# All down products moved behind the up products and put in seven-product form, with the tokens between them kept in DRAM

## The chip, the cores and the metric

The kernel runs on one core of a Trainium2 chip. The metric is the device time of one execution in microseconds (us), the median of the runs shown. Profiles are of one execution each, with times from the start of its span.

## The reference

Softmax attention with a tanh cap on the scores, over 4 batches, 12 heads, 448 tokens and heads of 64; then, per batch, a token mixing of rank 32 and a feed-forward layer 768 -> 3072 -> 768 with a relu.

```
scores = q @ k.T / 8;  scores = cap * tanh(scores / cap)
x = softmax(scores) @ v                     # heads side by side: 448 x 768 per batch
u = x + (x.T @ U @ V).T
out = u + relu(u @ w_ch1) @ w_ch2           # w_ch1 768 x 3072, w_ch2 3072 x 768
```

U, V, w_ch1 and w_ch2 come as 64-bit floats and are turned into 32-bit ones on the core (`convert`: one operation of ACT and two of DVE per block). Each 32-bit operand of the feed-forward layer is split in a high and a low half, and a product is the sum of three matmuls: high by high, high by low, low by high.

## The kernel before, in words

**Planning.** Every piece of work is a task with an estimated duration, the engines that may run it, the buffers that it takes and a priority (a lower number goes first). `simulate` (L133) places all tasks in time, an engine taking the ready task of the lowest number whose buffers have room, and `emit` (L230) writes the instructions out in that order, so each engine's order is fixed when the program is built. Buffers of one tag are handed out in the order in which they were declared, from the first of their pools that has room; a pool with `after` opens when all buffers that are to come from the named pools are done. `Pool.part` makes a pool out of one large tile of another.

**Attention** (`four`, `normalize`, `mixin`, to about 190 us). For each head pair `scores` (L488, PE), tanh (L495) and exp (L506, ACT), the product with v (L522, L531, L546), and DVE's sums of the exponentials over the key tiles (L552). The 448 keys are three tiles of 128 and a remainder of 64. Below head pair 12 (`ALONE`) the remainder is added into the sums by DVE; from 12 on PE adds it in a second set of matmuls with ones (L588). `fill` gives PE 14 small matmul turns (L405) at the start. Beside this the first feed-forward weights and the first token operands are made, as far as buffers allow: four token operands (tag `x`: one in `wx`, three in `xe`) and four weight operands (tag `ws` in `wp`).

**Feed-forward** (`moe`, L772). The batches are taken in two pairs, (0, 1) and (2, 3), each in 12 chunks of 256 hidden units. Up (`up_seven`): a chunk is a 2 x 2 block product (two batches by two blocks of 128 hidden units, the 768 inputs in two halves) done with seven products in place of eight, 9 matmuls of 448 columns each (L867): 63 per chunk. The products run in the order of `ORDER`; results are gathered in PSUM and in `cx` tiles by ACT (`keep`) and DVE (`plus`). Bank "a" takes products 1, 6, 7 and 4 one after the other, and is read in between.

Down, first pair (`down`): in plain form, 72 matmuls per chunk (L948), run between the up products of the next chunk, two outputs behind each product. The raw w1 and w2 of a chunk are loaded (L724, SP, 768 KB each, two buffers of tag `wr`), converted into `wa` tiles, written to DRAM for the second pair (L728, ACT's queue, 384 KB each), and split. Outputs go onto the result tiles `u` in SBUF by a DVE addition (L953), or, two in five, by a copy of ACT and an accumulating DMA of POOL's queue (L961).

Down, second pair: for ten of the twelve chunks, two chunks at a time, in seven-product form (`down_seven`, 126 matmuls, L1075), its operands made from the kept weights and from the relu'd tokens that stay in SBUF (tag `gq`); the last two chunks in plain form behind all up products. The 72 down products of the first pair's last chunk stand between the two pairs.

The operands of a pair (`operands`, L674) are seven tiles `x` of 6 rows x 448; terms 5, 6, 3 and 7 are formed in one `wr` buffer.

Of the kernel before, what the change touches and what calls it, by code (L numbers as in the profile page):

```python
# [29 lines left out]
QUADS = 5  # L30
PORDER = 2, 3, 1, 6, 5, 7, 4
# [6 lines left out]
FILL, FIRST = 14, 3  # L38
# [3 lines left out]
class Pool:  # L42


    def __init__(self, name, bufs, after=(), space=None, side=None, shared={}, within=None, parts=None):
        self.name, self.bufs, self.after, self.space, self.side = name, bufs, after, space, side
# [15 lines left out]
    def part(self, b, opened):  # L62
        if self.whole is None:
            p, g = self.within
            self.whole = opened(p).tile([128, NP, S], self.parts[0], tag=g, name=self.name, bufs=1)
        return self.parts[1][self.at(b)][b.slot](self.whole)
# [12 lines left out]
class Task:  # L79
    __slots__ = ("durs", "eng", "fn", "bufs", "prio", "mode", "lat", "wait", "next", "i", "begin", "at", "ready", "lock")  # L80
# [8 lines left out]
class Plan:  # L89
# [16 lines left out]
    def task(self, durs, fn, r=(), w=(), prio=0, mode=None, lat=None, begin=0, lock=False):  # L106
# [4 lines left out]
        t.lat, t.eng = lat, None  # L111
# [21 lines left out]
    def simulate(self):  # L133
# [6 lines left out]
        events, out, now = [], [], 0  # L140
# [34 lines left out]
        def start(t, e):  # L175
# [16 lines left out]
            heapq.heappush(events, (now + cost + OVER.get(e, 0) + (LAT[e] if t.lat is None else t.lat), 2, t.i, "d"))  # L192
# [37 lines left out]
    def emit(self, tc, order, first):  # L230

        engines = {"DVE": self.nc.vector, "POOL": self.nc.gpsimd, "ACT": self.nc.scalar}
        with tc.manual_schedule(), ExitStack() as st:

            def opened(p):
                if p.pool is None:
                    for q in p.after:
                        if q.stack:
                            q.stack.close()
                            q.stack = None  # L240
                    p.stack = st.enter_context(ExitStack())
# [28 lines left out]
class Build(Plan):  # L270
    def __init__(self, tc, qk, v, u, vv, w1, w2, cap, ident, out):
# [12 lines left out]
        self.xe = Pool("xe", {"x": 3, "cx": 2}, after=(self.pre,), shared={"st": "cx"})  # L284
# [4 lines left out]
        self.gx = [Pool("gx", {"g": 1}, after=(self.an, self.aq), within=w, shared={"gp": "g"}) for w in ((self.aq, "xx"), (self.an, "rb"))]  # L289
# [122 lines left out]
    def attention(self):  # L412
# [6 lines left out]
        self.gw = Pool("gw", {"gq": 3}, after=(self.wx,), within=(self.wx, "x"), parts=(F32, {"gq": thirds}))  # L419
        self.g0 = Pool("g0", {"gq": 3}, after=(self.ua,), within=(self.ua, "u0"), parts=(F32, {"gq": thirds}))  # L420
        self.gz = Pool("gz", {"gp": 3}, after=(self.g0,), within=(self.ua, "u0"), parts=(F32R, {"gp": thirds}))
        self.g1 = Pool("g1", {"gq": 1, "ta": 1, "vs": 1}, after=(self.ua,), within=(self.ua, "u1"), parts=(F32, {
            "gq": thirds, "ta": [lambda t: t[:, 2, :DM // 2]], "vs": [lambda t: t[:, 3:6]]}))
# [13 lines left out]
    def four(self, p):  # L437
# [73 lines left out]
        for h in range(2):  # L511
# [24 lines left out]
            for i, o in enumerate(os):  # L536
# [23 lines left out]
                if p < ALONE:  # L560
# [9 lines left out]
    def normalize(self, p):  # L570
# [5 lines left out]
        rest = p >= ALONE  # L576
# [97 lines left out]
    def operands(self, bs, order, prio):  # L674
# [3 lines left out]
        pools = (self.wx, self.xe, self.late) if bs[0] == 0 else (self.xe, self.late)  # L678
# [34 lines left out]
    def block(self, which, f, first, begin, prio):  # L713

        nc = self.nc
        a = self.buf("wa", [128, DM], F32, self.wp, self.late)
        if not first:
            self.task({"SP": 350}, lambda: nc.sync.dma_start(out=a.t, in_=self.kept[which, f]),
                r=[("kept", which, f)], w=[(a, 0)], lat=4000, prio=prio)
            return a  # L720
        raw = self.buf("wr", [128, 2 * DM], I32, self.wq)
# [4 lines left out]
        def keep():  # L726
            d = self.kept[which, f] = self.dp.tile([128, DM], F32, tag="kept", name="kept", bufs=2 * NF)
            nc.scalar.dma_start(out=d, in_=a.t)  # L728

        self.task({"SP": 350}, load, w=[(raw, "u"), (raw, "l")], lat=7500, prio=prio, begin=begin)  # L730
        self.convert(raw, lambda: raw.t, a, lambda: a.t, prio, DM)
        self.task({"ACT": 120}, keep, r=[(a, 0)], w=[("kept", which, f)], lat=7000, prio=prio)
        return a

    def strassen_weights(self, c, first, begin, prio):
# [3 lines left out]
        ws = {p: self.buf("ws", [128, 2, K], F32R, self.wp, self.late) for p in ORDER}  # L739
        c, c7 = (self.buf("ta", [128, K], F32, self.wp, self.g1) for _ in range(2))  # L740
# [9 lines left out]
    def weights(self, f, first, begin, prio):  # L750
        tag, pool = ("w1", self.wp) if first or f // CF != 2 * QUADS else ("wl", self.wq)
        w = self.buf(tag, [128, 2, DM], F32R, pool)
        a = self.block(1, f, first, begin, prio)

        def high():
            self.copy(self.nc.scalar, w.t[:, 0], a.t)

        def low(e):
            e.tensor_tensor(out=w.t[:, 1], in0=a.t, in1=w.t[:, 0].bitcast(F32), op=ALU.subtract)

        self.task({"ACT": 840}, high, r=[(a, 0)], w=[(w, 0)], prio=prio)
        self.task({"DVE": 960}, low, r=[(a, 0), (w, 0)], w=[(w, 1)], prio=prio, lock=True)
        return w

    def bank(self):
        return self.buf("mm", [128, 512], F32, self.pm, self.pl)

    def prepare(self, c, first, begin, prio):
        ws = self.strassen_weights(c, first, begin, prio)
        return ws, {c * CF + i: self.weights(c * CF + i, first, begin, prio) for i in range(CF) if first}  # L770

    def moe(self):  # L772


        self.kept, rest = {}, []
        order, pend = 10, None
        for n, bs in enumerate(((0, 1), (2, 3))):
            made = {}
            if not n:
                made[0] = self.prepare(0, True, 60000, ALONE - 90)  # L780
            xs = self.operands(bs, ORDER if n else EARLY, -50 if n else ALONE - 90)
            vs = self.buf("vs", [128, 3, S], F32, self.g1) if n else None
            gq, last, down, turns = {}, None, iter(()), [2] * 7
            for c in range(NCH):
                fs = [c * CF + i for i in range(CF)]
                ws, w1 = made.get(c) or self.prepare(c, n == 0, 0, 3 if n or c < NCH - 2 else -60)
                gs = {}
                four = n and c < 2 * QUADS
                if pend:
                    down, turns = self.down(order, *pend), [2] * 7  # L790
                    pend = None
                elif gq and c % 2 == 0:
                    down = self.down_seven(order, bs, c // 2 - 1, gq, vs)
                    gq = {}
                if n:
                    turns = [2] * 7 if not c else [1 + (i + c) % 2 for i in range(7)]
                if n and c == 0:
                    for _ in down:
                        pass
                    order += 12  # L800
                if four and c % 2 == 0:
# [360 lines left out]
```

## Time and profile before

| | us |
|---|---|
| three runs | 843.48, 842.36, 842.54; median 842.54 |
| profiled execution | 842.78, span 841.0 |

| engine | busy us | share |
|---|---|---|
| PE (matmuls) | 832.0 | 99% |
| PEld (weight loads, beside PE) | 663.2 | 79% |
| DVE | 675.6 | 80% |
| ACT | 498.2 | 59% |
| POOL | 123.5 | 15% |

The DMA engines moved 129.64 MB, 154 GB/s over the span. Busy times are of the engine's instructions and say nothing on what the end waits for; the chain of waits does, followed back from the last instruction. A mean duration in the lines is that of one instruction from start to end, and following instructions overlap a little with it; a list in order of time shows the step from one start to the next.

### The profile page before, as it was taken

The page shows a single profiled execution, that of the slowest core. Times are in us where ns is not written, and L with a number is a line of the kernel's source. Part 1 is how long each engine was busy: PE and PEld are TensorE (multiplying, and loading weights), DVE is VectorE, ACT ScalarE, POOL GpSimd, SP SyncE. Part 2 cuts the span into 40 slices and gives each one's busy share as a digit, 9 for nine tenths or more (in the row PEclk, how much of TensorE's full clock was granted, in tenths as well). Part 3 has the DMA queues.
Part 4 walks back from the last instruction along what each step waited for, and adds up shares of the span by engine and source line. Part 5 has one row for each costly group of instructions (what it writes and reads, how often), then busy time and mean ns, then how long its engine had stood idle before and what let it go on. Part 6 is the DMA issues. An engine that isn't in the chain of part 4 may idle for free.

```text
span 841.0 us, 12164 instructions
## 1 busy us (share of the span) xinstructions
PE 832.0 (99%) x4524; PEld 663.2 (79%) x4524; DVE 675.6 (80%) x1141; ACT 498.2 (59%) x748; POOL 123.5 (15%) x162
## 2 busy tenths in 40 slices
PE   9999999999999999999999999999999999999998
PEld 4343333337899999999999999999999999999997
DVE  4778999659878878887888899698797887978764
ACT  7989999876545544454455445365565555555510
POOL 0111111111111111111111112001121111211200
PEclk9999999999999999999999999999999999999999
DMA  6456554513878867867686747526346263642413
GB/s 228 132 158 208 152 179 121 168 46 117 254 217 220 262 198 216 237 189 214 205 266 160 207 102 192 148 60 157 71 97 152 44 157 78 134 108 44 103 32 131
DMA packets 47612, 129.64 MB, mean 154 GB/s; under 512 B 6178, under 2 KB 23618, under 8 KB 47554
## 3 DMA queue, kind: packets, MB, share of 16 engines
q1 hardware_dynamic: 23024, 79.29, 29.7%
q0 software_dynamic: 17616, 30.71, 20.1%
q10 hardware_dynamic: 6914, 18.88, 5.7%
q8 instruction: 35, 0.57, 0.3%
q14 instruction: 23, 0.19, 0.1%
HBM read 79.28 MB, written 24.47 MB: 123 GB/s over the span
## 4 chain that ended last, share of the span: by engine, by line
PE 95%; DVE 2%; DMA 1%; ACT 1%; issue 1%; POOL 0%; DVEq 0%; POOLq 0%; ACTq 0%
PE mm L867 36%; PE mm L948 24%; PE mm L1075 15%; PE sc L488 8%; PE o L546 6%; PE misc L662 1%; PE o L531 1%; PE misc L585 1%; PE misc L405 1%; DMA rd<-r 1%; PE misc L651 1%; PE misc L635 1%; DVE x L702 1%; DMA rb<-rd 0%; PE misc L588 0%
## 5 line engine op out<-in xcount | busy, mean ns | idle before, releaser
L867 PE MATMUL mm<-x,ws 128*128 128x448 f32 x1512 | 330.7, 366 | 0.8 <-ACT cx L263 0.8
L867 PEld LDWEIGHTS mm<-x,ws 128*128 128x128 f32 x1512 | 283.3, 188 | 27.5 <-ACT cx L263 1.8
L948 PE MATMUL mm<-g,w 128*128 128x448 f32 x864 | 187.0, 366 | 0.0
L948 PEld LDWEIGHTS mm<-g,w 128*128 128x128 f32 x864 | 162.1, 188 | 13.8 <-issue 0.2
L1075 PE MATMUL mm<-g,w 128*128 128x448 f32 x630 | 139.2, 366 | 0.0
L1075 PEld LDWEIGHTS mm<-g,w 128*128 128x128 f32 x630 | 118.3, 188 | 9.7
L263 ACT ACTIVATE st<-mm 128x448 f32<-128x448 f32 x109 | 59.2, 543 | 80.7 <-PE mm L948 48.7
L961 POOL DMA_DIRECT2D u<-st x60 | 51.7, 862 | 272.3 <-ACT st L263 272.3
L953 DVE TENSOR_TENSOR u<-u,mm 128x448 f32<-128x448 f32 x108 | 66.1, 618 | 29.3 <-PE mm L948 28.9
L488 PE MATMUL sc<-qk 64*128 64x448 f32 (+1 forms) x384 | 77.4, 571 | 0.4 <-ACT th L495 0.4
L506 ACT ACTIVATE th<-th,capt 128x1792 f32<-128x1792 f32 x42 | 75.3, 1792 | 0.8
L495 ACT ACTIVATE th<-sc 128x896 f32<-128x896 f32 x80 | 69.6, 915 | 5.1 <-PE sc L488 4.9
L1098 POOL DMA_DIRECT2D u<-st x45 | 38.9, 864 | 211.6 <-ACT st L263 174.1
L488 PEld LDWEIGHTS sc<-qk 64*128 64x128 f32 (+1 forms) x384 | 27.6, 175 | 41.3 <-issue 18.1
L546 PE MATMUL o<-th,vn 128*64 128x448 f32 x280 | 57.9, 548 | 0.0
L263 ACT ACTIVATE cx<-mm 128x448 f32<-128x448 f32 x42 | 22.9, 546 | 57.4 <-PE mm L867 49.3
L702 DVE TENSOR_TENSOR ws<-ta,ws 128x384 fp32r<-128x384 f32 x96 | 52.8, 554 | 3.1 <-ACT ws L263 2.2
L263 ACT ACTIVATE ws<-ta 128x384 fp32r<-128x384 f32 x57 | 29.5, 520 | 34.6 <-PE mm L867 22.6
L317 DVE SCALAR_TENSOR_TENSOR wa<-wa,wr 128x768 int32<-128x768 int32 (+2 forms) x50 | 46.6, 932 | 4.0 <-ACT wa L309 3.3
L263 ACT ACTIVATE ws<-wa 128x384 fp32r<-128x384 f32 x51 | 26.0, 520 | 39.5 <-PE mm L867 39.5
L552 DVE TENSOR_TENSOR es<-es,th 128x896 f32<-128x896 f32 (+1 forms) x36 | 39.1, 1086 | 11.6 <-ACT th L506 10.9
L309 ACT ACTIVATE wa<-wr 128x768 f32<-128x768 f32 (+2 forms) x50 | 44.3, 888 | 6.9 <-DVE cx L880 1.9
(123 smaller groups left out, 932.3 us busy)
## 6 DMA issues: line engine op xcount, KB each, us to landing
wr<-in_w SPq DMA_DIRECT2D x48, 768.0 KB, 6.7
u<-st POOLq DMA_DIRECT2D x105, 224.0 KB, 4.2
kept<-wa ACTq DMA_DIRECT2D x48, 384.0 KB, 6.4
wa<-kept SPq DMA_DIRECT2D x28, 384.0 KB, 3.7
qk<-in_qk SPq DMA_DIRECT2D x23, 448.0 KB, 4.1
wr<-kept SPq DMA_DIRECT2D x20, 384.0 KB, 4.0
vn<-in_v SPq DMA_DIRECT2D x12, 448.0 KB, 3.9
rb<-rd POOLq DMA_DIRECT2D x24, 224.0 KB, 3.8
```

The costliest lines, as they stand in the source:

```text
L263: e.activation(out=out, in_=in_, func=func)
L317: nc.vector.scalar_tensor_tensor(out=a_t().bitcast(I32), in0=a_t().bitcast(I32), scalar=3, in1=raw_t()[:, 0::2], op0=ALU.logical_shift_lef ...
L488: nc.tensor.matmul(ps.t[out, a, :S], qks[c].t[hd, 1, 128 * t:min(S, 128 * t + 128)], qks[c].t[hd, 0], start=True, stop=True)
L495: nc.scalar.activation(out=th.t[:, j], in_=ps.t[:, :, :S], func=AF.Tanh, scale=(self.half if t == 3 else self.qsc) if raw else 1.0)
L506: nc.scalar.activation(out=th.t, in_=th.t, func=AF.Exp, scale=self.capt)
L546: nc.tensor.matmul(o.t[64 * a:64 * a + 64, :S], vn.t[:, 3 * i + t, a], th.t[:, j, a], start=False, stop=t == 2)
L702: e.tensor_tensor(out=lo, in0=src(), in1=hi.bitcast(F32), op=ALU.subtract)
L867: nc.tensor.matmul(ps.t[:, :S], ws[p].t[:, wi, sl], xs[p].t[:, xi, d], start=fresh and n == 0, stop=n == 8, skip_group_check=not fresh)
L948: nc.tensor.matmul(ps.t[:, :S], w1[f].t[:, wi, sl], g[b, f].t[:, gi], start=f == fs[0] and i == 0, stop=f == fs[-1] and i == 2)
L953: nc.vector.tensor_tensor(out=u.t[:, d], in0=u.t[:, d], in1=ps.t[:, :S], op=ALU.add)
L961: nc.gpsimd.dma_start(out=u.t[:, d], in_=st.t, accum_op=ALU.add)
L1075: nc.tensor.matmul(ps.t[:, :S], w[:, wi, k, sl], g[gi][:, k], start=fresh and n == 0, stop=n == 5, skip_group_check=not fresh)
```

## The change

The feed-forward layer has three stages: all up products of the first pair, all up products of the second pair, and then all down products. The relu'd tokens of both pairs are written to DRAM (`mid`, 224 KB per block, POOL's queue) and read back in the down stage. Down goes over three groups of two sets of four blocks (512 hidden units each); in a group each of the seven products is done for both pairs and three output tiles, 12 matmuls each, all in seven-product form. The raw down weights are converted at places set by `SECONDS`: 4 blocks in the first stage, 12 in the second, 8 in the first down group; they are kept in DRAM in another layout (`quads`). Product 5, which belongs to two outputs, is added to both. Every third output goes by ACT and an accumulating DMA.

Before a chunk's last up product (4) the next chunk's first (5) is put by its priority. The remainder of the softmax sums is added by DVE throughout (`RESTS`), the warm-up turns are 11, attention's early pool `pre` has seven score buffers for three. A pool `wg` opens when `pre` is done and holds two more weight buffers and a large tile, in which the fifth token operand lies (`bx`) and later two down weights (`bw`). The planner counts the transfers' time by size (`moved`).

```
-QUADS = 5
-PORDER = 2, 3, 1, 6, 5, 7, 4
+GROUPS = (0, 1), (2, 3), (4, 5)
+EVERY = 3
+SECONDS = (0, 0, 1, 0, 1, 0, 1, 0, 1, 0, 0, 0), (0, 0, 1, 1, 1, 1, 1, 2, 1, 2, 1, 1), (2, 2, 2, 2)
+PORDER = 2, 1, 3, 6, 5, 7, 4
 ALONE = 12
-FILL, FIRST = 14, 3
+RESTS = 24
+FILL, FIRST = 11, 3
...
@@ simulate
+            if t.size:
+                self.moved = max(self.moved, now + cost + 1800) + t.size
+                done = max(done, self.moved + 500)
...
-        self.wp = Pool("wp", {"wa": 2, "w1": 3, "g": 3, "ws": 4, "ta": 3}, shared={"gp": "g"})
+        self.wp = Pool("wp", {"wa": 2, "ws": 4, "ta": 3})
-        self.pre = Pool("pre", {"th": 3, "qk": 2, "es": 2})
+        self.pre = Pool("pre", {"th": 7, "qk": 2, "es": 2})
+        self.wg = Pool("wg", {"big": 1, "wb": 2, "g": 3}, after=(self.pre,), shared={"wa": "wb", "ws": "wb"})
+        self.bx = Pool("bx", {"x": 1}, after=(self.pre,), within=(self.wg, "big"), ...)
+        self.bw = Pool("bw", {"wl": 2}, after=(self.bx,), within=(self.wg, "big"), ...)
...
+        self.wc = Pool("wc", {"wb": 4}, after=(self.late,), within=(self.wp, "ws"))
+        self.wt = Pool("wt", {"wt": 2}, after=(self.late,), within=(self.wp, "wa"))
+        self.cl = Pool("cl", {"gq": 9, "st": 2}, after=(self.xe,))
+        self.cr = Pool("cr", {"wb": 4, "wt": 2, "wl": 1, "wr": 1, "wa": 1, "gq": 2, "g": 4}, after=(self.late,), side="right")
...
@@ four
-                if p < ALONE:
+                if p < RESTS:
@@ normalize
-        rest = p >= ALONE
+        rest = p >= RESTS
...
@@ moe
+                prio = 3 if n or c < NCH - 2 else -60
+                ws = ws or self.strassen_weights(c, n == 0, 0, prio)
+                for _ in range(SECONDS[n][c]):
+                    self.block(1, next(seconds), True, 0, 3)
+                self.up_seven(n, c, xs, ws, order)
+                ws = None
+                order += 21
+        self.down_all(order, seconds)
...
@@ up_seven
+        if not begin:
+            at = iter([order - 4, *at][:1] + list(range(order + 3, order + 21, 3)))
+        cx = {x: self.buf("cx", [128, S], F32, self.xe, *self.rows) for x in ("c22", "c11", "c12")}
...
+        def store(b, j, x):
+            at = n, c // 2, b, j
+            def out():
+                if at not in self.mid:
+                    self.mid[at] = self.dp.tile([128, 2, S], F32, tag="mid", name="mid", bufs=2 * NF)
+                nc.gpsimd.dma_start(out=self.mid[at][:, c % 2], in_=to(x))
+            self.task({"POOL": 1000}, out, r=[key(x)], w=[("mid", at, c % 2)], lat=4000, size=620, prio=-200)
...
@@ down_all
+        for ms in GROUPS:
+            for x, p in enumerate(PORDER):
+                for _ in range(SECONDS[2][x - 3] if ms is GROUPS[0] and x > 2 else 0):
+                    self.block(1, next(seconds), True, 0, prio, (self.cr,))
+                for m in ms:
...
+                    if p == 3:
+                        term(a[m, 1, 0], a[m, 0, 0], ALU.subtract, a[m, 1, 0], size)
+                        s2[m] = self.buf("wt", [128, 2, K], F32, self.wt, self.cr)
+                        term(s2[m], a[m, 1, 1], ALU.subtract, a[m, 1, 0], size)
+                    if p in (3, 5):
+                        ts = self.buf("wt", [128, 2, K], F32, self.wt, self.cr)
...
+                    x = w[p, m] = self.buf("wl", [128, 2, 2, K], F32R, self.bw, self.wq, self.cr)
+                    split(...)
+                for n in range(2):
+                    for m in ms:
+                        at = {2: (1, 0), 3: (1, 1), 1: (0, 0), 6: (0, 1), 7: (1, 0)}.get(p)
+                        if at:
+                            b[(m, n, *at)] = token(m, n, *at)
+                        if p == 6:
+                            term(b01, b11, ALU.subtract, b01, size)
+                            term(b00, b01, ALU.add, b00, size)
+                        if p == 5:
+                            term(b11, b11, ALU.subtract, b00, size)
+                        if p == 7:
+                            term(b10, b10, ALU.subtract, b00, size)
+                        hi, lo = g[p, n, m] = [self.buf("g", [128, 2, S], F32R, self.wg, *self.gx, self.cr) for _ in range(2)]
+                        split(src, ...)
+                for n, bs in enumerate(((0, 1), (2, 3))):
+                    for d in range(3):
+                        fresh = p not in (6, 5, 4)
...
+                        self.task({"PE": 6 * 206 * len(ms)}, products, ..., prio=order, mode="mm")
+                        order += 1
+                        for u, e in onto:
+                            count += 1
+                            self.onto(ps, ..., count % EVERY == 0 and not (last and p in (7, 4)))
```

`split` makes the high half on ACT and the low half on DVE; `term` is one DVE operation; `token` and `weight` are loads on SP's queue.

## Rows read from the trace of the kernel before

**Rows 1.** Span of the core and mean granted clock (1 is full speed).
```profile
core 0: 841.0 us, clock 0.999
```
**Rows 2.** The chain of work that ended last, by engine.
```profile
PE 95%; DVE 2%; DMA 1%; ACT 1%; issue 1%; POOL 0%; DVEq 0%; POOLq 0%; ACTq 0%
```
**Rows 3.** Stretches: PE, PEld, DVE, ACT, POOL busy (instructions), clock, DMA share, GB/s.
```profile
20.00:140.00 120.00, 117.35 (x848) 43.48 (x844) 103.07 (x158) 113.90 (x122) 18.96 (x31) 1.00 0.53 159
...
100.00:191.00 91.00, 90.36 (x681) 33.96 (x685) 70.98 (x114) 80.03 (x86) 14.08 (x24) 1.00 0.42 125
...
260.00:280.00 20.00, 20.00 (x100) 18.35 (x99) 16.17 (x28) 10.17 (x19) 2.59 (x3) 1.00 0.94 274
...
480.00:500.00 20.00, 20.00 (x101) 18.54 (x100) 19.65 (x39) 10.92 (x21) 2.58 (x3) 1.00 0.57 140
...
520.00:540.00 20.00, 20.00 (x101) 18.51 (x99) 12.38 (x24) 7.42 (x14) 2.58 (x3) 1.00 0.82 241
```
**Rows 4.** The chain in order of time: start us, us, what.
```profile
234.92 3.70 PE mm L867 x18
...
482.52 3.66 PE mm L867 x18
...
526.34 27.43 PE mm L867 x135
...
807.93 29.11 PE mm L948 x144
```
**Rows 5.** DVE in order of time: start us, us, line, operation, shapes, count.
```profile
205.33 0.61 DVE L880 TENSOR_TENSOR cx<-cx,mm 128x448 f32<-128x448 f32 x1
205.87 0.55 DVE L695 TENSOR_TENSOR ta<-wa,ta 128x384 f32<-128x384 f32 x1
206.33 0.55 DVE L314 TENSOR_SCALAR wr<-wr 128x768 int32<-128x768 int32 x1
206.80 0.61 DVE L835 SCALAR_TENSOR_TENSOR g<-cx,g 128x448 fp32r<-128x448 f32 x1
207.62 1.09 DVE L614 TENSOR_TENSOR u<-u,rb 128x896 f32<-128x896 f32 x1 [0.21 <-DMA rb<-rd]
208.63 0.55 DVE L702 TENSOR_TENSOR ws<-ta,ws 128x384 fp32r<-128x384 f32 x1
...
213.56 0.97 DVE L317 SCALAR_TENSOR_TENSOR wa<-wa,wr 128x768 int32<-128x768 int32 x1
214.44 0.96 DVE L759 TENSOR_TENSOR w<-wa,w 128x768 fp32r<-128x768 f32 x1
215.31 1.15 DVE L669 TENSOR_TENSOR u<-u,misc 128x448 f32<-128x448 f32 x2
```
**Rows 6.** Groups by line: busy us, mean ns | idle before, releaser.
```profile
L961 POOL DMA_DIRECT2D u<-st x60 | 51.7, 862 | 272.3 <-ACT st L263 272.3
...
L309 ACT ACTIVATE wa<-wr 128x768 f32<-128x768 f32 (+2 forms) x50 | 44.3, 888 | 6.9 <-DVE cx L880 1.9 <-DVE wa L317 1.7 <-DVE ws L702 1.6
...
L263 ACT ACTIVATE g<-gw 128x896 fp32r<-128x896 f32 x19 | 18.0, 948 | 1.5 <-DVE gw L994 1.3
...
L588 PE MATMUL misc<-th,ones 128*32 128x448 f32 x48 | 5.6, 539 | 0.0
```
**Rows 7.** DMA queues (q1 SP, q0 POOL, q10 ACT): packets, MB, share of 16 engines.
```profile
q1 hardware_dynamic: 23024, 79.29, 29.7%
q0 software_dynamic: 17616, 30.71, 20.1%
q10 hardware_dynamic: 6914, 18.88, 5.7%
```
**Rows 8.** The chain's last piece: start us, us, what.
```profile
837.07 0.62 DVE u L953
```
**Rows 9.** Raw weight loads (L724): landing; SP's waits for a buffer (total, times, longest).
```profile
DMA to landing us min/median/max: 5.2/6.7/8.3
...
SPq L724 <- DVE wa L317: 218.7, 45, 12.3
```

More of the change, by code (lines that the diff above doesn't have):

```diff
@@ L139, in simulate @@
         locked = {"DVE": 0, "POOL": 0}
-        events, out, now = [], [], 0
+        events, out, now, self.moved = [], [], 0, 0
         for t in self.tasks:
@@ L240, in opened @@
                             q.stack = None
+                    for q in p.under:
+                        opened(q)
                     p.stack = st.enter_context(ExitStack())
@@ L711, in part, with block @@
         self.task({"DVE": 130 + 1.09 * n}, partial(low, src=src), r=[k, (t, 2 * d)], w=[(t, 2 * d + 1)], prio=prio, lock=True)
-    def block(self, which, f, first, begin, prio):
+    def block(self, which, f, first, begin, prio, only=None):
         nc = self.nc
-        a = self.buf("wa", [128, DM], F32, self.wp, self.late)
+        a = self.buf("wa", [128, DM], F32, *(only or (self.wp, self.late, self.wg)))
         if not first:
-            self.task({"SP": 350}, lambda: nc.sync.dma_start(out=a.t, in_=self.kept[which, f]),
-                r=[("kept", which, f)], w=[(a, 0)], lat=4000, prio=prio)
+            self.task({"SP": 350}, lambda: nc.sync.dma_start(out=a.t, in_=self.kept[f]),
+                r=[("kept", which, f)], w=[(a, 0)], lat=4000, size=1200, prio=prio)
             return a
-        raw = self.buf("wr", [128, 2 * DM], I32, self.wq)
+        raw = self.buf("wr", [128, 2 * DM], I32, *(only or (self.wq,)))
         def load():
@@ L748, in strassen_weights @@
         return ws
[L750 to L763, printed above, removed]
@@ L765, in bank @@
     def bank(self):
         return self.buf("mm", [128, 512], F32, self.pm, self.pl)
-    def prepare(self, c, first, begin, prio):
-        ws = self.strassen_weights(c, first, begin, prio)
-        return ws, {c * CF + i: self.weights(c * CF + i, first, begin, prio) for i in range(CF) if first}
     def moe(self):
-        self.kept, rest = {}, []
-        order, pend = 10, None
+        self.kept, self.quads, self.mid = {}, {}, {}
+        order, seconds = 10, iter(range(NF))
         for n, bs in enumerate(((0, 1), (2, 3))):
-            made = {}
-            if not n:
-                made[0] = self.prepare(0, True, 60000, ALONE - 90)
+            ws = None if n else self.strassen_weights(0, True, 60000, ALONE - 90, (self.wg,))
@@ L823, in moe @@
-        self.last_sums(bs, vs)
-        for x in rest:
-            for _ in self.down(order, *x):
-                pass
-            order += 20
-    def relu(self, b, f, src, key, gs):
-        nc = self.nc
-        tag, pools = ("g", (self.wp, *self.gx)) if b < 2 else ("gp", (self.gz, self.wp, *self.gx))
-        g = gs[b, f] = self.buf(tag, [128, 2, S], F32R, *pools)
-        def low():
-            nc.vector.scalar_tensor_tensor(
-                out=g.t[:, 1], in0=src(), scalar=0.0, in1=g.t[:, 0].bitcast(F32), op0=ALU.max, op1=ALU.subtract)
-        self.task({"ACT": 550}, lambda: self.copy(self.nc.scalar, g.t[:, 0], src(), AF.Relu), r=[key], w=[(g, 0)], prio=-200)
-        self.task({"DVE": 640}, low, r=[key, (g, 0)], w=[(g, 1)], prio=-200)
@@ L905, in up_seven @@
             result(0, 1, "c12")
-            yield
         else:
```

329 lines of the change are left out of this document (100 added, 229 removed).

## The prediction

> **What bounds the kernel now.** I read the views in this order: span and clock, the chain that ended last, the stretches, then the lines and queues that the new stages lean on. The one core takes 841.0 us at a granted clock of 0.999 of full speed [rows 1], so no part of the time is a clock to be won back. The chain of waits is TensorE for 95% [rows 2]. The stretches say the same of the feed-forward part: PE is busy for 20.00 of 20 us with its weight loads at 18.35 to 18.54, while DVE runs from 12.38 to 19.65 of 20 [rows 3]. So what counts there is the number of matmuls times their pitch. The pitch is read from the chain: from 234.92 to 482.52 us lie nine chunks of 135 matmuls (63 up, 72 down), 247.60 / 1215 = 0.2038 us each; a stretch of up products alone gives 27.43 / 135 = 0.2032, the last stretch of down products 29.11 / 144 = 0.2022 [rows 4]. I take 0.2035. That the 135 up products at 526.34 run without a gap and with no down work between them matters for the change: it is the form of its first two stages, though with the weights already in 32 bits.
>
> The attention part (to about 196 us, which is 837.07 less 3150 x 0.2035) is less clear: from 20 to 140 us PE is busy 117.35 of 120 us and ACT 113.90 [rows 3].
>
> The profiled execution took 842.78 us, 1.8 us more than its span; the median of the three runs is 842.54, so both are one number for this purpose. A measurement of this kernel can tell about 0.2% (1.7 us) from no change.
>
> **The matmuls.** Before: up 24 x 63 = 1512; down 12 x 72 = 864 in plain form for the first two batches, 5 x 126 = 630 in seven-product form and 2 x 72 = 144 plain for the others: 3150. After: up 1512 again; down 3 groups x 7 products x 6 outputs x 12 matmuls = 1512: 3024. That removes 126 x 0.2035 = 25.6 us, all of it on the path.
>
> **The attention.** With RESTS at 24 the sums of the remainder rows leave PE: six normalizations lose their second half, whose 48 instructions take 5.6 us [rows 6], some 5.2 us without the overlap of their ends. DVE takes 12 more additions of 896 elements, at 1.01 us each when they follow one another [rows 5] 12.1 us; a fifth token operand (three low halves, 1.6 us) and two weight operands (about 1.9 us) come forward as well, while the two down weights that were converted and split there (2 x 2.2 us) go. Net about 11 us on a DVE that is busy 70.98 of the 91 us from 100 to 191 [rows 3]: it fits. ACT there is at 80.03 of 91. I count the 5.2 us as gained; the bounds are 0 (ACT or DVE takes the place) and 7.2 (the four extra score buffers also remove some 2 of the 2.65 us in which PE idles from 20 to 140 us). Three warm-up turns fewer lie in PE's idle time: nothing, at most 1 us.
>
> By PE's busy share this stage is PE's. The Trainium skill (Perfetto Trace Analysis, Identifying the Most-Contended Engine) holds matmul busy time to be a bad measure and takes the share of weight-load time in its place; by it PE, with 43.48 of 120 us of weight loads here, would not be the bound, ACT at 113.90 would, and the 5.2 us would be worth nothing: 821 us in place of 816. The trace sides with neither wholly, and the case is a rival below.
>
> **First stage: up products of the first pair, no down work between.** A chunk now lasts 63 x 0.2035 = 12.8 us where it lasted 27.5. DVE per chunk, with the steps from one start to the next [rows 5]: two raw blocks 2 x (0.47 + 0.88) = 2.7, four terms and seven low halves 11 x 0.46 = 5.1, three additions 3 x 0.54 = 1.6, a third of a down-weight conversion 0.45: 9.8 of 12.8 us, 77%. That is less than the 19.65 of 20 at 480 us, beside which PE had no gap. The transfers are nearer to their limit. The queues' bytes over their share of the span give 317 GB/s for SP's, 394 for ACT's, 182 for POOL's, which mostly accumulates [rows 7]. Per chunk: two raw blocks of 768 KB 5.0 us, two kept blocks 2.0, a third of a down weight 1.2, and the four stores of relu'd tokens (0.92 MB), an operation that before doesn't have: at ACT's rate 2.3, at POOL's own 5.0. So 10.5 us (82%) or 13.2 us (103%) of 12.8. Before loads the engines to 0.94 of their time in one stretch [rows 3] with PE at 20.00. A plain store has no read of its destination, so I take 2.3; the other end costs at least 0.4 x 11 = 4 us, and more through latency (a rival). POOL issues four stores per chunk at 862 ns [rows 6]: 3.4 of 12.8 us.
>
> The relu'd low halves and plain down weights that go (four and two per 27.5 us) were DVE and ACT work under PE: nothing.
>
> The last product of a chunk writes the bank that an addition of DVE still reads. Down products stood between; now the next chunk's first product does (1.83 us). An operation under way (up to 1.09) and the addition (0.61) [rows 5] make 1.7 us, ahead of what the signals take. I take 0; without that cover it would be 1 us per chunk.
>
> **The seams.** Into the second pair, the 72 down products at 511.77 that covered the new token operands are gone. Two of the seven fit in the spare buffers; five are left, 24 operations x 0.54 = 12.9 us of DVE, with 7 to 10 weight operands (7.4) and six additions (3.2): 23.5 us in the 20 us between the first freed buffer and the last product that needs one. Up to 3 us late, 0 where weights are ready early; I take 2. At the start, chunk 1 now comes 12.8 us after chunk 0, and one raw buffer is held by the token term until its seventh operand: 1. Into the down stage, the last buffers open only when up ends, but three tokens and five operand buffers lie ready, which is half a product, 7.3 us; what is missing is one load, at most the 8.3 us that the longest landing of a larger one took [rows 9], and two splits: 1. In all 4, bounds 0 and 8.
>
> **Down stage.** Per group DVE does 22 weight operations (768 elements) x 0.87 = 19.1, 44 token operations (896) x 1.01 = 44.4, and 32 of 48 evictions x 0.54 = 17.3: 80.8 us beside 504 x 0.2035 = 102.6 us of PE, 79%; the first group converts eight more down weights, 8 x 1.35, 89%. The heaviest products, 6 and 5, take 18.7 and 18.5 us there against 14.7, so they must be prepared ahead; the terms are formed in place in the 14 token buffers, for which products 2 and 1 (8 us each) leave room. I take 0. The end is as before: an eviction of 0.62 [rows 8] and a store.
>
> **Sum.** 842.8 - 25.6 - 5.2 + 4 = 816 us.
>
> **Rivals.**
> (a) Attention gives nothing back, because ACT or the fuller DVE sets it: 821, up to 825 where DVE's 11 us don't all fit. For it: ACT at 95% from 20 to 140 us. Against: from 100 to 191, where the sums go, PE has 90.36 of 91 and ACT 80.03 [rows 3].
> (b) The loop of raw weights sets the first stage. Two buffers serve 2.33 loads per chunk, so one turn may last 11.0 us. It needs a landing, 5.2 to 8.3 us now with a median of 6.7, then ACT's 0.89 and DVE's 0.95 with an operation ahead of each, some 3 us [rows 5, 6, 9]. The 45 waits of SP for a free buffer, 218.7 us, show that it now turns at leisure, 13.8 us [rows 9]. With 8.3 + 3.7 = 12.0 each of some 26 loads costs half a microsecond more: 13 us, 829 us.
> (c) Slower than before: the same loop with landings that grow with the queue, since 3.7 MB in 12.8 us is 286 GB/s, above all that the stretches show (274 at 0.94). At 11 us plus 3 a turn is 14, a chunk 16.3, and 11 chunks cost 39 us: 855. It decides from landings of about 10.1 us (a turn of 13.1, 27 us lost). Against: nothing above 8.3 was seen.
> (d) The ring of nine operand buffers paces the down stage. Half a product (7.3 us of PE) frees four; if terms are not made ahead, product 6 needs ACT 0.95 [rows 6], two low halves 2.0, a weight's 0.9, two evictions 1.1 and four terms 4.0: 9.0 us. With product 5 at 8.9 that is 6.6 us per group, 20 in all, and 7 more for the eight conversions: 843, no change. Against: 14 token buffers let the terms run ahead.
>
> **How the numbers follow.** Forecast 0.60, with 809 to 824 as its own range; (a) 0.12, (b) 0.12, (c) 0.10, (d) 0.06. The 80% range is 809 to 836: it takes in (a) and (b) and leaves out (c) and (d). Faster: 0.60 + 0.12 + 0.12 + a part of (d) = 0.86; the same: the middle of (d), 0.03; slower: (c) and the rest of (d), 0.11.
>
> **What would show it.** PE: 3024 matmuls at 0.203 us. First stage: products back to back, 12.8 us per chunk; DMA share about 0.8, raw landings under 8 us; gaps in PE with raw weights as releaser would show (b) or (c). Attention: first up product about 5 us earlier and no second half of the sums. Seams: single gaps of 1 to 3 us at some 345 and 500 us. Down: PE at 20.00 of 20, DVE at 16 to 18; gaps ahead of products 6 and 5 would show (d). The prediction is wrong if PE has more than 10 us of gaps after the attention, or a pitch other than 0.203.

## The result, and the profile after

The changed kernel takes 828.99 us (median of four runs, 828.35 to 829.72) beside 842.45 (four runs, 841.5 to 843.48): a ratio of 0.984, 95% interval 0.9823 to 0.9857. It is 13.5 us (1.6%) faster, where the forecast was 26.5 us faster, at 816.0. The profiled execution took 828.35 us with a span of 826.6 at a granted clock of 0.993 (before [rows 1]: 841.0 at 0.999).

Stretches of after ("after" is the changed kernel, "before" the other), columns as in [rows 3]:
```profile
20.00:185.00 165.00, 159.53 (x1150) 58.29 (x1148) 144.14 (x216) 154.39 (x169) 25.05 (x42) 1.00 0.46 139
185.00:220.00 35.00, 30.39 (x186) 22.95 (x183) 26.64 (x49) 18.27 (x37) 5.59 (x10) 0.90 0.53 177
220.00:340.00 120.00, 119.39 (x586) 109.30 (x585) 107.05 (x205) 73.22 (x132) 21.57 (x37) 1.00 0.79 275
340.00:380.00 40.00, 39.29 (x193) 35.76 (x192) 39.67 (x83) 25.63 (x50) 7.18 (x12) 1.00 0.57 190
380.00:490.00 110.00, 110.00 (x545) 101.91 (x543) 87.37 (x177) 55.70 (x100) 20.22 (x35) 1.00 0.76 254
490.00:520.00 30.00, 25.75 (x118) 22.79 (x117) 12.42 (x18) 12.11 (x20) 4.47 (x8) 0.94 0.47 168
520.00:620.00 100.00, 100.00 (x493) 92.19 (x492) 95.12 (x117) 48.69 (x65) 14.24 (x16) 1.00 0.92 296
620.00:820.00 200.00, 200.00 (x984) 184.57 (x983) 155.16 (x187) 77.55 (x105) 24.09 (x28) 1.00 0.50 134
```
The first number after the comma is PE. The three long stretches of the feed-forward part (220 to 340, 380 to 490, 520 on) are full, but for 0.61 us in the first. PE is missing in two short ones: 4.61 us from 185 to 220 and 4.25 from 490 to 520, and both have a granted clock below full speed. Attention has lost something too: 5.47 us of idle PE from 20 to 185, where before had 165 - 162.35 = 2.65:
```profile
20.00:185.00 165.00, 162.35 (x1188) 59.92 (x1186) 133.99 (x205) 153.26 (x162) 25.47 (x42) 1.00 0.49 146
```

The end of the chain of waits of after (start us, us, what), which answers to [rows 4, 8], without the steps of `issue` (0.02 to 0.04 us each) and one eviction of 0.63 us:
```profile
355.25 151.67 PE mm L817 x747
507.62 2.10 PE mm L817 x9
509.74 3.54 DMA wb<-quad
513.30 0.85 ACT bw L272
514.18 0.97 DVE bw L908
515.19 307.70 PE mm L963 x1504
```
The pitch is 151.67 / 747 = 0.2030 us for up products. For down products it is 307.70 / 1504 = 0.2046 (eight of the 1512 ran before), or 0.2036 without some 1.5 us at a lower clock at its start. Between them lies a seam of 8.3 us in which 9 + 6 + 2 matmuls ran; a load of a down weight, its high half (L272) and its low half (L908) stand in the chain there. The load starts 0.02 us after the last up product ends, and SP's longest wait ahead of such a load (total, times, longest, us) was for an up product:
```profile
SPq L889 <- PE mm L817: 16.8, 2, 13.6
```
So the buffer that this down weight needed was held by an up weight until then. The end of the kernel is an eviction of 0.62 us, as it was.

PE in order of time at the start of the feed-forward part, after (start us, us, line, operation, shapes, count, idle time before it and its releaser):
```profile
198.63 2.09 PE L817 MATMUL mm<-x,ws 128*128 128x448 f32 x9
205.27 1.10 PE L650 MATMUL misc<-ident,u 64*112 64x64 f32 x16 [4.55 <-DVE u L629]
206.30 3.73 PE L817 MATMUL mm<-x,ws 128*128 128x448 f32 x9
209.96 1.08 PE L666 MATMUL misc<-xx,ust 112*32 112x128 f32 x16
210.97 2.08 PE L817 MATMUL mm<-x,ws 128*128 128x448 f32 x9
```
After 4.55 us without work, nine matmuls take 3.73 us, where they take 2.09 ahead of the hole and 2.08 a little later: the granted clock is 0.50 from 206 to 210 us, the lower of its two levels (1.2 GHz, not 2.4). With the transposes (1.10 for 0.66) and the 16 mixing products (1.08 for 0.65), that is another 2.5 us, so this hole costs some 7.

What DVE, ACT and POOL did around it, same columns, from three views of after:
```profile
204.12 1.09 DVE L629 TENSOR_TENSOR u<-u,rb 128x896 f32<-128x896 f32 x1 [2.25 <-DMA rb<-rd]
```
```profile
204.44 0.55 ACT L272 ACTIVATE cx<-mm 128x448 f32<-128x448 f32 x1 [4.33 <-DMA mid<-cx]
```
```profile
196.84 1.05 POOL L624 DMA_DIRECT2D rb<-rd  x2 [2.35 <-DMA rd<-r]
197.88 0.57 POOL L843 DMA_DIRECT2D mid<-cx  x1
```
Two things come late at once. The last normalization (L629) waits for its reciprocals, a DMA issued at 196.84, and PE's order has its transposes ahead of further up products. Beside that, ACT cannot copy an up product out of PSUM, since both `cx` tiles are held: ACT's wait ends with the landing of a store that was issued at 197.88, and the copy starts at 204.44.

POOL's DMA queue in after, which answers to [rows 7], and landing times of the raw weights and the new store (issue, count, KB each, median us):
```profile
q0 software_dynamic: 14400, 37.82, 17.1%
```
```profile
wr<-in_w SPq DMA_DIRECT2D x48, 768.0 KB, 6.5
mid<-cx POOLq DMA_DIRECT2D x96, 224.0 KB, 4.3
```
By these POOL's queue moves 37.82 MB in 17.1% of 826.6 us, 268 GB/s, where it gave 182 while mostly accumulating. In the first stage PE was busy 119.39 of 120 us with the DMA share at 0.79; raw weights landed at a median of 6.5 us.

### The profile page after: what moved, and what is told of

It is laid out like the page before. It is cut to its first block, busy times and chain, and to the rows that moved or that the text cites. A ratio compares the mean times of both kernels' runs of the same rounds, so it can differ in the third digit from the quotient of the medians.

```text
span 826.6 us, 11913 instructions
## 1 busy us (share of the span) xinstructions
PE 805.9 (97%) x4344; PEld 639.0 (77%) x4344; DVE 676.8 (82%) x1067; ACT 481.1 (58%) x686; POOL 123.0 (15%) x193
## 3 DMA queue, kind: packets, MB, share of 16 engines
q0 software_dynamic: 14400, 37.82, 17.1%
## 4 chain that ended last, share of the span: by engine, by line
PE 59%; DVE 2%; DMA 1%; issue 0%; ACT 0%; ACTq 0%
PE mm L963 37%; PE mm L817 22%; DMA wr<-in_w 1%; DVE cx L830 0%; DMA wb<-quad 0%; DVE x L717 0%; DVE wr L710 0%; ACT wa L328 0%; DVE ta L710 0%; DVE bw L908 0%; ACT bw L272 0%; DVE ws L717 0%; DVE u L983 0%; DVE wr L333 0%; DVE x L274 0%
## 5 line engine op out<-in xcount | busy, mean ns | idle before, releaser
L963 PE MATMUL mm<-g,bw 128*128 128x448 f32 x756 | 176.1, 368 | 3.5 <-ACT bw L272 3.3
L963 PE MATMUL mm<-g,wl 128*128 128x448 f32 x756 | 174.0, 365 | 0.0
L963 PEld LDWEIGHTS mm<-g,bw 128*128 128x128 f32 x756 | 142.3, 188 | 16.2 <-ACT bw L272 3.6
L963 PEld LDWEIGHTS mm<-g,wl 128*128 128x128 f32 x756 | 142.6, 189 | 12.1 <-issue 0.2
L272 ACT ACTIVATE st<-mm 128x448 f32<-128x448 f32 x44 | 24.0, 546 | 142.4 <-issue 91.7
L843 POOL DMA_DIRECT2D mid<-cx x96 | 55.6, 580 | 258.2 <-ACT cx L272 252.7
L272 ACT ACTIVATE cx<-mm 128x448 f32<-128x448 f32 x96 | 48.9, 543 | 61.7 <-PE mm L817 44.5
L908 DVE TENSOR_TENSOR g<-gq,g 128x896 fp32r<-128x896 f32 x62 | 67.1, 1085 | 11.1 <-ACT g L272 10.1
L988 POOL DMA_DIRECT2D u<-st x44 | 38.3, 871 | 245.3 <-ACT st L272 229.1
L272 ACT ACTIVATE g<-gq 128x896 fp32r<-128x896 f32 x62 | 57.6, 944 | 12.0 <-PE mm L963 9.8
L830 DVE TENSOR_TENSOR cx<-cx,mm 128x448 f32<-128x448 f32 x72 | 44.4, 616 | 20.9 <-PE mm L817 16.4
L567 DVE TENSOR_TENSOR es<-es,th 128x896 f32<-128x896 f32 (+1 forms) x48 | 51.9, 1081 | 11.5 <-ACT th L521 11.0
L272 ACT ACTIVATE cx<-cx 128x448 f32<-128x448 f32 x72 | 41.6, 577 | 31.4 <-DVE cx L830 30.7
```

The lines of the kernel that those rows point to most:

```text
L272: e.activation(out=out, in_=in_, func=func)
L567: e.tensor_tensor(out=out(), in0=in0(), in1=in1(), op=ALU.add)
L843: nc.gpsimd.dma_start(out=self.mid[at][:, c % 2], in_=to(x))
L908: self.task({"DVE": 130 + 1.09 * size}, lambda: nc.vector.tensor_tensor(out=lo(), in0=src.t, in1=hi().bitcast(F32), op=ALU.subtract), r=[( ...
L963: nc.tensor.matmul(ps.t[:, :S], w[p, m].t[:, wi, k, sl], g[p, n, m][gi].t[:, k], start=fresh and i == 0, stop=i == len(at) - 1, skip_group ...
```

## The experiments

The theories on record are these. For the hole at 201 us: (A) a copy finds no `cx` tile, as a store still holds it; (B) the late normalization alone. After runs 1 to 4 it became: both at once, so that only both edits together close it (run 5). For the seam at 507: (C) the first down weights need a slot of `wb` that an up weight still holds; (D) down operands come late whatever holds the slots. For attention, which gave back less than forecast: (E) ACT alone sets it; (F) PE itself does; (G) the longer queue of DVE holds PE back. The kernel before, run beside them, took 842.27 us (runs 1 to 4), 842.18 (5 to 7) and 841.87 (8 to 10, one execution). One caution holds for the first six: the kernel's order is worked out anew when a cost or a pool changes, so an edit moves other instructions as well. The last four keep the order of after.

**1. The last normalization's turn is given later.**
```diff
- lat=7800 if p == 1 else 5000 if p < 20 else 3800, prio=prio)
+ lat=7800 if p == 1 else 5000 if p < 20 else 3800 if p < 23 else 8000, prio=prio)
```


> Edit: the last normalization's broadcast is given a longer latency (8000 for 3800) in the planner, so that PE's order has the last head pair's transposes behind four more up products; other places of the plan shift with it, the head of the down stage among them. Theory A (the hole of 4.55 us in PE at 201 us is held by the copy of product 6, which finds no tile because the first output's store to DRAM still holds it): the hole stays, 3 to 5 us, now ahead of an up product and behind ACT's copy. Rival B (the hole is the late normalization alone, and PE runs on once the transposes stand later): no hole over 1 us at 201. In both, the hole of 3.3 us at 511 goes, since the second down weight gets its buffer in this plan, with up to 2.8 us in the first down group instead. Time: A 824 to 827 us, B 818 to 821 us.

826.99 us (825.76 to 827.32), ratio 0.9814 [0.9799, 0.9829]. PE in order of time, this kernel:
```profile
204.77 8.10 PE L817 MATMUL mm<-x,ws 128*128 128x448 f32 x27 [4.36 <-ACT cx L272]
212.80 0.66 PE L650 MATMUL misc<-ident,u 64*112 64x64 f32 x16
```
The transposes come later and wait for nothing, and the hole is still there, as (A) has it, now with the copy `cx` as its releaser. So the two causes lie side by side: in the order of after the transposes wait 4.55 us for the normalization, in this one the products wait 4.36 for the copy. The 27 matmuls after it take 8.10 us in place of 5.7. In this order the down seam is gone (PE 30.00 of 30 from 490 to 520), though the slots are shared as before; 2.4 us are idle from 380 to 490 instead, behind copies.

**2. A third `cx` tile, paid for with a late weight operand and a token buffer.**
```diff
- self.xe = Pool("xe", {"x": 3, "cx": 2}, ...
+ self.xe = Pool("xe", {"x": 3, "cx": 3}, ...
- self.late = Pool("late", {"x": 4, "ws": 3, "wa": 1}, ...
+ self.late = Pool("late", {"x": 4, "ws": 2, "wa": 1}, ...
- self.cr = Pool("cr", {..., "gq": 2, "g": 4}, ...
+ self.cr = Pool("cr", {..., "gq": 1, "g": 4}, ...
```


> Edit: a third tile for up outputs in the pool xe (three for two), paid with one weight operand less in the late pool and one token buffer less in the down stage; the normalization's latency is left. Theory A: PE runs product 7 ahead of the transposes, the hole at 201 us goes (under 1 us) and with it the half clock behind it, together 7 us; some of it comes back at the seam into the second pair (about 355 us), where the operands' DVE work then lies bare for 3 to 5 us. Rival B: the hole at 201 us stays over 3 us, as the transposes still wait for the normalization. Hole at 511: gone in this plan in both, with about 1 us in the first down group. Time: A 819 to 823 us, B 825 to 828 us.

830.64 us (830.29 to 831.29), ratio 0.9861 [0.9846, 0.9876]: the time missed the expectation, the place did not. PE in order of time:
```profile
199.43 5.73 PE L817 MATMUL mm<-x,ws 128*128 128x448 f32 x27
...
206.21 0.66 PE L650 MATMUL misc<-ident,u 64*112 64x64 f32 x16 [1.04 <-DVE u L629]
...
358.13 17.07 PE L817 MATMUL mm<-x,ws 128*128 128x448 f32 x75 [3.87 <-DVE ws L717]
```
With the tile, 27 matmuls run at full speed where the copy had stopped them, and 1.04 us is left ahead of the transposes. What was won is paid back at the second pair: PE waits 3.87 us for a weight operand, 4.7 us are idle from 340 to 380, where the granted clock is 0.96. The wait is for an operand of the kind that was given up, though no run gives that buffer back by itself.

**3. The up weights no longer share the slots of `wb` for the whole second stage.**
```diff
- ws = {p: self.buf("ws", [128, 2, K], F32R, self.wp, self.wg, self.late) for p in ORDER}
+ ws = {p: self.buf("ws", [128, 2, K], F32R, *((self.wp, self.wg, self.late) if first else (self.wp, self.late))) for p in ORDER}
```


> Edit: in the second stage the up weights' operands no longer use the two buffers of the pool wg, which the first down weights need. Theory C (the hole at 511 us is the wait for the second of the first two down weights, whose buffer an up weight held until the end of the stage): that hole of 3.3 us and the low clock behind it go, 4 to 6 us; at most 1.2 us near 485 and 2.8 us in the first down group come instead; the hole at 201 stays as it is. Rival D (down operands come late at the seam whatever holds the buffers, because loads and splits start only when up ends): a hole of 3 us or more stays at the seam. Time: C 823 to 826 us, D 828 to 830 us.

827.01 us (826.16 to 827.82), ratio 0.9817 [0.9802, 0.9831]. Stretches as in [rows 3]:
```profile
380.00:490.00 110.00, 107.88 (x531) 99.07 (x530) 82.10 (x161) 57.96 (x106) 19.33 (x35) 1.00 0.72 244
490.00:520.00 30.00, 30.00 (x150) 27.76 (x149) 17.21 (x31) 12.55 (x22) 4.51 (x8) 1.00 0.48 163
520.00:620.00 100.00, 98.86 (x485) 90.31 (x484) 94.22 (x117) 49.21 (x65) 14.11 (x16) 1.00 0.92 304
```
The seam is full, as (C) has it. That alone is no proof, since runs 1, 2 and 4 lost the seam too, by their new orders; the wait of SP in after is the direct sign of the shared slot. 2.1 us are now idle in the second stage, which has fewer weight operands, and 1.1 in the down stage, so the kernel gains 2.0 us over after and not the 5.7 of the seam. It fell short of the expected 823 to 826.

**4. The remainder sums go back to PE.**
```diff
-RESTS = 24
+RESTS = 12
```


> Edit: the remainder of the softmax sums goes back to PE from head pair 12 on, as in the kernel before. As forecast (the move is worth all of PE's 5.2 us): the first up product starts 4 to 5 us later than the changed kernel's 185.5 us. Rival E (ACT sets attention, the move is worth nothing): it starts within 1 us of 185.5. Halfway (the 2.4 us that the two traces show): 187 to 189. The hole at 511 goes in this plan with up to 2.8 us in the first down group, so the whole time says little on attention alone: 827 to 830 us as forecast, 823 to 825 by rival E.

824.24 us (820.93 to 826.18), ratio 0.9784 [0.9751, 0.9816]: 4.7 us faster than the change as it stands, though the first up product starts at 187.09 and not 185.52: what the expectation calls halfway. The hole at the start stays at 4.45 us; the down seam is gone in this order. So what the edit costs in attention was outweighed by what the new order saved behind it, and the run does not price the sums by themselves.

**5. Both causes of the start hole taken away, the sums on PE.**
```diff
-RESTS = 24
+RESTS = 12
- self.wg = Pool("wg", {"big": 1, "wb": 2, "g": 3}, ...
+ self.wg = Pool("wg", {"big": 1, "wb": 2, "g": 2}, ...
- self.xe = Pool("xe", {"x": 3, "cx": 2}, ...
+ self.xe = Pool("xe", {"x": 3, "cx": 3}, ...
- lat=7800 if p == 1 else 5000 if p < 20 else 3800, prio=prio)
+ lat=7800 if p == 1 else 5000 if p < 20 else 3800 if p < 23 else 6000, prio=prio)
```


> Edit: a third tile for up outputs, paid with one operand buffer of the down stage (wg g 2 for 3) in place of a weight operand; the last normalization's latency 6000 for 3800, so that its transposes stand later in PE's order; the remainder sums of softmax back on PE from head pair 12 on. Theory A (the hole at 201 us has two causes at once, the tile held by a store and the late normalization, so only both edits together close it): PE's idle time from 185 to 220 us falls from 4.6 to under 1.5 and the clock stays full there, 5 to 7 us; no hole at 511 in this plan. Rival B (one cause is left, the transfers all land late there): a hole of 3 us or more stays. Time: A 815 to 819 us; B 822 to 825.

**816.08 us** (815.1 to 816.5), ratio 0.9689 [0.9676, 0.9703]: faster than both kernels. Stretches as in [rows 3]:
```profile
185.00:220.00 35.00, 34.11 (x221) 25.41 (x218) 29.98 (x57) 19.15 (x38) 5.95 (x11) 1.00 0.66 213
...
490.00:520.00 30.00, 30.00 (x150) 27.80 (x149) 17.15 (x26) 13.55 (x21) 4.82 (x8) 1.00 0.57 191
520.00:620.00 100.00, 99.40 (x490) 91.49 (x489) 98.18 (x122) 49.04 (x64) 13.18 (x16) 1.00 0.92 302
```
The tile is paid for with one of the nine operand buffers `g` of the down stage, which runs on with eight (99.40 of 100), and not with one that the second pair needs. The start has 0.9 us idle where it had 4.61, the clock is full there, and the other seams have none (40.00 of 40 from 340 to 380). Its first up product is at 187.58, 0.36 us ahead of before: this kernel is the matmul term alone (842.2 - 25.6 = 816.6), with next to nothing from attention and next to nothing lost at seams. No run has the third tile and the late turn with the sums left on DVE, so what the move of the sums is worth without the hole stays open.

**6. The same with half of the sums on PE** (`RESTS = 18`; here the remainder of head pairs 18 and 19 is counted twice).

> As the last, but the remainder sums go to PE only from head pair 18 on (the changed kernel: never; the one before: from 12). If ACT and PE bound the attention together, so that moving the sums is worth some 2 us for six normalizations, this one lies 0.5 to 1 us under the last: 814 to 818. If the move is worth PE's 5.2 us in full: 2.6 us under it. If it is worth nothing: equal.

818.36 us (814.49 to 819.71), ratio 0.9721 [0.9708, 0.9734]. Its runs spread over 5 us, so it cannot be ranked against the fifth run: inconclusive.

**7 to 10. What sets attention, in the order of after.** 7 leaves out the exp of one head of each pair (less work for ACT), 8 is after itself, 9 leaves out most of the 12 additions that DVE got (their first 32 of 448 columns stay), 10 does both.
```diff
  # 7 and 10
- nc.scalar.activation(out=th.t, in_=th.t, func=AF.Exp, scale=self.capt)
+ nc.scalar.activation(out=th.t[:, :, 0], in_=th.t[:, :, 0], func=AF.Exp, scale=self.capt)
  # 9 and 10
- some = lambda es=es, rows=rows: es.t[rows]
+ n = S if p < ALONE else 32
+ some = lambda es=es, rows=rows, n=n: es.t[rows, :, :n]
```


> The changed kernel with exp taken of one head of each pair alone (the other keeps its tanh), so that ACT does about 36 us less in attention while the order on every engine is the same; the output is not softmax's. Theory E (ACT sets the pace of attention in the changed kernel, which is why taking the remainder sums off PE gave 2 us and not 5): the first up product starts 3 us or more ahead of 185.5. Rival F (PE sets it, and ACT's load is beside the point): within 1.5 us of 185.5. The rest of the run is as the changed kernel's.

> The changed kernel itself once more, beside the next two, for the spread of the start of its first up product from run to run (185.2 to 186.5 us in the runs so far with the same attention). Expected: 185 to 187, the whole run 828 to 830 us.

> The changed kernel with the 12 additions that the move gave to DVE cut to 32 of 448 columns, so that DVE does some 10 us less from 100 to 190 us and the order on every engine is the same; the softmax sums of the later head pairs lack most of their remainder. Theory G (the longer queue of DVE holds PE back in attention: PE's copies, sums and mixing steps wait behind those additions, so that of PE's 5.2 us only some 2 came through): the first up product starts 2 to 3 us ahead of the run beside it, at 183 to 184. Rival F (PE's own pace, whatever ACT and DVE do): within 0.7 us of it.

> Both cuts: the 12 additions at 32 of 448 columns and exp on one head of each pair alone, with the order unchanged. If ACT and DVE each take the other's place: 2 to 4 us ahead of the unchanged kernel, where neither alone gives it. If PE's own pace and the order hold it: within 1 us.

The times of single executions were 828.31, 829.47, 829.39 and 827.74 us, within 0.6 us of what after takes; all four have the start hole (4.5 to 4.8 us) behind attention. What tells is attention itself. First how full the engines are from 100 to 185, columns as in [rows 3], in this order: after, runs 7, 9 and 10.
```profile
100.00:185.00 85.00, 81.73 (x610) 30.07 (x612) 79.29 (x120) 79.74 (x90) 12.30 (x21) 1.00 0.44 131
100.00:185.00 85.00, 82.60 (x614) 30.45 (x614) 79.34 (x123) 67.92 (x90) 13.02 (x22) 1.00 0.45 136
100.00:185.00 85.00, 82.41 (x612) 30.02 (x612) 69.86 (x120) 79.65 (x90) 12.47 (x22) 1.00 0.45 131
100.00:185.00 85.00, 84.31 (x624) 31.30 (x621) 71.99 (x126) 68.54 (x91) 13.92 (x24) 1.00 0.46 136
```
PE had 84.36 here in before and 80.82 in run 8. With ACT relieved of 12 us alone, or DVE of 9 us alone, it gets a part of that back; with both, 84.31.

The start of the first up product says less than it seems to. The five kernels with unchanged attention (after, runs 1, 2, 3 and 8) have it from 185.2 to 186.9, and half of that spread is there at 24 us. Run 7 has it at 186.46, but it lost time ahead of all this, in a hole behind DVE that is twice as long as in after (0.96 us), with a lower clock behind it (the twelve score products take 1.83 us in after):
```profile
76.86 1.02 PE L677 MATMUL misc<-vst,ys 64*128 64x448 f32 x4 [1.92 <-DVE ys L274]
77.71 2.92 PE L503 MATMUL sc<-qk 64*128 64x448 f32 x12
```
Run 10 has the same hole. So I count from the seventh of the twelve sums, the first to have had a second half on PE in before. PE's seventh sums and first up product, in this order: before, after, runs 7, 9 and 10.
```profile
115.03 0.96 PE L585 MATMUL misc<-es,ones 128*32 128x448 f32 x8
187.94 2.09 PE L867 MATMUL mm<-x,ws 128*128 128x448 f32 x9
113.44 0.96 PE L600 MATMUL misc<-es,ones 128*32 128x448 f32 x8
185.52 2.08 PE L817 MATMUL mm<-x,ws 128*128 128x448 f32 x9
114.52 0.96 PE L600 MATMUL misc<-es,ones 128*32 128x448 f32 x8
186.46 2.09 PE L817 MATMUL mm<-x,ws 128*128 128x448 f32 x9
113.03 0.96 PE L601 MATMUL misc<-es,ones 128*32 128x448 f32 x8
185.15 2.09 PE L818 MATMUL mm<-x,ws 128*128 128x448 f32 x9
114.49 0.96 PE L601 MATMUL misc<-es,ones 128*32 128x448 f32 x8
184.16 2.09 PE L818 MATMUL mm<-x,ws 128*128 128x448 f32 x9
```
From the one to the other the five kernels with unchanged attention take 72.1 to 72.9 us (after 72.08, run 8 72.87). Run 7 takes 71.94 and run 9 72.12: relieving either engine alone gives nothing that can be told from that spread, so neither (E) nor (G) holds by itself. Run 10 takes 69.67, some 2.5 us less: both together hold PE back, against (F). The chain of waits from 100 to 186 says who stands in: in run 7 DVE's additions (L567) with 20.2% of it, in run 9 ACT's tanh and exp with 14.0 and 14.6%. How DVE and ACT divide the loss stays open; runs 7, 9 and 10 are one execution each.

## Why the prediction was right and wrong

The direction and the largest term held, and half of the gain came. What was mis-sized is the seams, and to a smaller part attention. Against the forecast span of 816 - 1.8 = 814.2 us, after has 12.4 too many: 9.5 at the seams, 2.4 in attention, 0.6 in the first stage.

The measured 829 lies outside the forecast's own range, 809 to 824, to which I gave 0.60. The 80% range, 809 to 836, holds it only because it was stretched for rivals (a) and (b); (b) even names 829, but what (b) describes did not happen, and (a) accounts for 2.4 us. That the wide range holds the number is luck.

**The matmuls** (-25.6): right. The pitch of 0.203 to 0.204 held in all stages, and the fifth run, with hardly a seam left and attention as before, is 26.1 us faster than before.

**The first stage** (no loss): right. 119.39 of 120 us with a DMA share of 0.79, forecast some 0.8, and raw landings under 8 us at the median. Rivals (b) and (c) did not occur. The sum of (b) was not sound either: it adds 3.7 us to a landing where its text finds some 3; with 3 a turn is 11.3 us, and (b) comes to about 820 and not 829. The longest landing, 11.1 us, is above the 8.3 of [rows 9] and cost no visible gap. The new store takes 580 ns of issue on POOL, under the 862 taken for it; at its queue's 268 GB/s, four of them are 3.4 us per chunk, between the 2.3 chosen and the other end, 5.0.

**The down stage** (no loss): right. 300.00 of 300 us from 520 to 820, so rival (d) did not occur. DVE was fuller in its first part than forecast, 95.12 of 100 us and not 89%, and still in time.

**The seams** (+4, bounds 0 to 8): the term of the sum that failed, with about 13.5 us.
- Start: 1 forecast, some 7 measured (4.55 idle and 2.5 of lower clock). I looked for weights and raw buffers there. What came late was the last normalization. From its sums to its DVE step it takes 16.6 us (187.54 to 204.12), no longer than before (189.96 to 207.62); but PE has 45 up products in that time, where before had 63 and 6 down products. Beside it came the `cx` tiles, which the new store holds until it lands. The prediction priced that store in issue time and bytes, not in how long it holds the tile.
- Second pair: 2 forecast, 0.7 measured.
- Into down: 1 forecast, 5.7 measured: 0.71, 3.26 and 0.28 of idle PE and about 1.5 of lower clock. I had written that one load was missing, at most 8.3 us, with half a product ready to cover it. One of the two first down weights was not ready, so its load and its split came in series after the last up product, as its slot was held by an up weight until then (SP's wait of up to 13.6 us for an up product; run 3, where the slot is not shared, has no seam).

The lower clock after a hole was in no term: in before, at 0.999, PE waits for nothing longer than 1.2 us at a time, and I read its clock as "no part of the time is a clock to be won back".

**Attention** (-5.2): too large. The first up product is at 185.52 (before 187.94, so 2.4 earlier; by the mean of the five kernels with this attention 1.9), and the sixth second half of the sums, which stood behind it, is gone (0.9): about 2.8 us. And half of that is not from the moved sums. At the seventh sums, ahead of the first half that was moved, after already leads by 1.6 us (113.44 to 115.03), and runs 4 and 5, with the sums on PE, lead there too (112.89 and 113.82); of the fewer warm-up turns, the score buffers and the new order no run says which did it. The stretch behind, which lost five halves of some 0.87 us each (4.3), takes 72.3 us by the mean of the five kernels, where before takes 72.9 and runs 4 and 5 take 74.2 and 73.8: of the 4.3 between 0.6 and 1.9 came. My "it fits" took DVE and ACT one at a time. Run 10 beside 7 and 9 shows that, with DVE at 79 and ACT at 80 of 85 us, the two together hold PE back by some 2.5 us. Rival (a) held in part.

The Trainium skill (Perfetto Trace Analysis, Identifying the Most-Contended Engine) takes the engine with the highest occupancy as the bound, and PE's weight-load share in place of its matmul time; by it ACT would be the bound and the move, as I worked it out, worth nothing. The trace agrees in that most of the 4.3 us did not come, and differs in that ACT relieved alone gave nothing (71.94 us beside 72.08).

By my own last test the prediction is wrong if PE has more than 10 us of gaps after attention. It has 4.61 + 0.61 + 0.71 + 4.25 = 10.2, just over, so by that test it was wrong.

## What to carry to other kernels

When covering work is taken out at a stage's edge, go through every producer chain that ends at that edge (each DMA in it at its measured landing) and every buffer that a store or another stage still holds there; a store's price is also the time it keeps its source. An engine with room by itself may have none beside a second full engine, when both sit in the same chain. A buffer that closes one hole is only free if it does not come from a stage that uses it: of two ways to pay for the same tile, one lost 1.7 us against after and the other, with the late turn and the sums on PE as well, won 12.9.

## What the runs showed of the hardware that was not expected

A hole of about 4.4 us in PE costs some 2.5 us more than itself: nine matmuls took 3.73 us after it in after, 27 took 8.10 in run 1, at a granted clock of 0.83 from 200 to 220 us in both. A hole of 1.04 us in run 2 was followed by transposes at 0.66 us, the full-speed value. But the hole of 1.92 us in run 7, among attention's small matmuls (PE busy 2.08 of the 4 us from 74 to 78), was followed by a granted clock of 0.57 from 78 to 82.

The transfers can run fuller than the 0.94 at 274 GB/s of [rows 3]: in the stretch of after from 520 to 540 us (columns as there) the share is 1.05 at 379 GB/s, with PE without a gap. (A share above 1 also says that it is not exact.)
```profile
520.00:540.00 20.00, 20.00 (x101) 18.49 (x100) 17.84 (x22) 9.95 (x13) 2.65 (x3) 1.00 1.05 379
```
